# Attention feeding a feed-forward layer: one transposition earlier, one pair of loads swapped, one accumulation order regrouped

## The chip, the cores and the metric

The kernel runs on one core of one Trainium2 chip. The metric is the device time of one execution in microseconds (us). Three runs of the kernel before took 290.9, 291.38 and 291.52 us, median 291.38 us. The profiled execution of it spans 289.5 us; all times "at so many us" below are counted from the start of that span. The TensorE clock granted during it was 1.0 of full speed throughout.

Engine names as the profile gives them: PE is TensorE (matrix multiplication), PEld its weight loads, DVE is VectorE, ACT is ScalarE, POOL is GpSimd, SP is SyncE. SPq and POOLq stand for the queues from which transfers are issued.

## What is computed

Eight batches of attention with pooled keys and values, and then a feed-forward layer over all 4608 tokens:

```python
# q, k, v: 8 batches x 8 heads x 576 tokens x 64, float32
k_p = k.reshape(B, H, 72, 8, 64).mean(axis=3)      # 8 neighbours pooled: 72 keys
v_p = v.reshape(B, H, 72, 8, 64).mean(axis=3)
attn = softmax(q @ k_p.T / 8)                      # 576 x 72 for each head
x = (attn @ v_p)                                   # laid out as 4608 tokens x 512
h = x @ w_in                                       # 512 -> 2048
out = (h * sigmoid(h)) @ w_out                     # 2048 -> 512, float32
```

## The kernel before

The tokens are worked in nine **tiles** of 512 tokens, t = 0 to 8; attention is worked in eight **batches** of 576 tokens. In tile t the feed-forward layer is computed (`up`: the first product and the activation, then `down` or `down_quarters`: the second product), and batch a = t + 1 of the attention is slipped in between its matmuls. What is slipped in are "fillers": pairs of a step number and a function, where step i is the i-th matmul (or pair of matmuls) of the stage.

```python
def spread(fillers, n):
    todo = sorted(fillers, key=lambda f: f[0])
    for i in range(n):
        yield i                                  # the caller issues matmul i here
        while todo and todo[0][0] <= i:          # then the fillers due at step i
            todo.pop(0)[1]()
```

The order in which the program issues instructions is the order in which each engine gets them[...].

The second product of the first tile (t = 0) is plain. Its 512 tokens are four groups m = 0 to 3 of 128, with one PSUM bank for each group, and there are three such banks (`mm=3`), so groups 0, 1, 2 go together and group 3 takes the bank that group 0 leaves:

```python
def down(t, fillers, ms):                        # ms = [(0, 1, 2), (3,)]
    step = spread(fillers, KG * sum(len(mm) for mm in ms))      # KG = 16
    for mm in ms:
        o_ps = [ps_tile([128, d_model], FP32, "mm", "o_ps") for m in mm]
        for g in range(KG):                      # g: 16 slices of the 2048 hidden units
            for m, ps in zip(mm, o_ps):
                next(step)
                nc.tensor.matmul(ps, lhsT=h_T[:, g, m * 128 : (m + 1) * 128],
                                 rhs=w_out_sb[:, g, :],
                                 start=(g == 0), stop=(g == KG - 1))
        for m, ps in zip(mm, o_ps):
            copy = nc.vector.tensor_copy if m == 1 else nc.scalar.copy
            copy(o_sb[m // 2][:, m % 2, :], ps)
            store(t, m, slice(0, d_model))       # 4 transfers on SyncE's queue
```

Its fillers, by step of the 64 matmuls, are the attention of batch 1 (`a = 1`), and sums of weights for the later tiles:

```python
sc_at, den_at, nu_at = (1, 16, 30), (16, 30, 44), (44, 55, 56)   # t == 0
# scores: 16 matmuls, then 4 Exp on ACT;  denominators: 4 matmuls, then Ln, Exp on ACT
# numerators: 32 matmuls, then 2 multiplications on DVE that write xT for the next tile
f_down.append((37 + 3 * j, lambda j=j: select_v(1, j, "at")))    # 6 matmuls, j = 0, 1
f_down.append((37 + 3 * j, lambda j=j: copy_v(1, j)))            # 1 copy on DVE
# steps 48 to 55: weight_sum(1, ...) and weight_sum(3, ...), 8 additions on DVE
```

From t = 1 on the second product takes seven quarter products in place of eight (Strassen's scheme, in the variant of Winograd) and needs sums of hidden units on DVE:

```python
def down_quarters(t, fillers, last=False):       # 112 steps
    product(2, KA, KQ); product(5, KA, KQ); product(2, 0, KA)   # steps 0 to 23
    nc.scalar.copy(r_sb, ps["P"])
    product(5, 0, KA)                                           # steps 24 to 31
    tt(out=rr_sb, in0=ps["Q"], in1=r_sb, op=add)
    product(1, 0, KQ, cc)                                       # steps 32 to 47
    tt(out=t_sb[:, cs], in0=ps["R"][:, cs], in1=rr_sb[:, cs], op=sub)
    ...                                          # products 4, 3, 7 and 6, with copies and stores
```

The queries are transposed by four instructions of DVE for each batch, one for each half of the heads (n % 2) and half of the tokens (n // 2). In tile 1 three of them are in `up`, the fourth in `down_quarters`. It is needed by the scores of the second third of the tokens, at step 31:

```python
q_at = [15, 16, 17, 8] if t > 1 else [24, 25, 26, 8] if t else [82, 84, 86, 88]
for n in range(4):
    f_to = f_down if t and n == 3 else f_up
    f_to.append((q_at[n], lambda n=n: q_transpose(a, n % 2, n // 2)))
sc_at, den_at, nu_at = (1, 31, 75), (31, 56, 97), (56, 97, 101)        # t > 0
```

In tile 1 the values of batch 2 are pooled by six instructions of DVE (`slot_sums`, each half: two additions and one that writes the bf16 result), at step 8 as well, and issued ahead of the transposition because they were listed first. They are used at step 40:

```python
elif t == 1:
    for j in range(2):
        ...
        f_down.append((8, lambda j=j: slot_sums("v", j, halves=True)))
        f_down.append((40, lambda j=j: select_v(2, j, "at")))
        f_down.append((41, lambda j=j: copy_v(2, j)))
```

Batches 3 to 7 have their keys and values loaded in two parts: `load_one` writes the first four tokens of each eight through SyncE's queue, and `load_rest` adds the other four on top of it through GpSimd's queue, once the first part has landed. The queries go through GpSimd's queue, behind one another in the order of issue:

```python
elif a + 1 < B:                                            # t = 1 to 5
    f_up.append((0, lambda: load_q(a + 1)))                # nc.gpsimd.dma_start
    f_up.append((1, lambda: load_one(a + 1, "k")))         # nc.sync.dma_start, two of them
    f_up.append((2, lambda: load_rest(a + 1, "k")))        # nc.gpsimd.dma_start, adding
    f_down.append((11, lambda: load_one(a + 1, "v")))
    f_down.append((12, lambda: load_rest(a + 1, "v")))
```

Of the kernel before, what the change touches and what calls it, by code (L numbers as in the profile page):

```python
# [36 lines left out]
def kernel(  # L37
# [9 lines left out]
    nc = tc.nc  # L47
# [5 lines left out]
    d_model = H * D  # L53
    d_ff = moe_w_in.shape[1]
    KF = d_model // 128
    KG = d_ff // 128
# [118 lines left out]
    def load_one(b, name):  # L175
        st = batches.setdefault(b, {})
        raw = raw_tile(f"{name}_raw", H)
        load_rows(nc.sync, raw, source(b, name)[:, :, :PH])
        st[f"{name}_raw"] = raw
# [374 lines left out]
    def store(t, m, cs, engines=(nc.sync,)):  # L554
        n0 = (t * NTT + m * 128) // QP
        src = o_sb[m // 2][:, m % 2, cs]
        if n0 // QI == B - 1:
            engines[0].dma_start(out=out[n0 * QP : n0 * QP + 128, cs], in_=src)
            return
        for u in range(128 // QP):  # L560
            n = n0 + u
            rows = (
                out[n * QP : (n + 1) * QP] if n // QI == B - 1
                else out_r[n // QI, n % QI]
            )
            engines[u % len(engines)].dma_start(
                out=rows[:, cs], in_=src[QP * u : QP * (u + 1)]
            )


    def down(t, fillers, ms):
        step = spread(fillers, KG * sum(len(mm) for mm in ms))
        for mm in ms:
            o_ps = [ps_tile([128, d_model], FP32, "mm", "o_ps") for m in mm]
            for g in range(KG):
                for m, ps in zip(mm, o_ps):
                    next(step)
                    nc.tensor.matmul(  # L578
                        ps,
                        lhsT=h_T[:, g, m * 128 : (m + 1) * 128],  # L580
                        rhs=w_out_sb[:, g, :],
                        start=(g == 0), stop=(g == KG - 1),
                    )
            for m, ps in zip(mm, o_ps):
                copy = nc.vector.tensor_copy if m == 1 else nc.scalar.copy
                copy(o_sb[m // 2][:, m % 2, :], ps)  # L586
                store(t, m, slice(0, d_model))
        for _ in step:
            pass

# [194 lines left out]
    for t in range(NT):  # L785
        a = t + 1
        f_up, f_down = [], []
        if t == 0:
            GA = 11
            items = [(g, 0, HS) for g in range(GA)]  # L790
            items += [(g, HS, NTT - HS) for g in range(GA)]
            items += [(g, 0, NTT) for g in range(GA, KG)]
            f_up += [(1, lambda: denominators(0, part(0, 1), on_dve=True))]
            f_up += [(5, lambda: denominators(0, part(1, 1), on_dve=True))]
            f_up += [(13, lambda: numerators(0, part(0, 1)))]
            f_up += [(17, lambda: numerators(0, part(1, 1)))]
        else:
            G = lambda *gs: [(g, 0, NTT) for g in gs]
            if t == 1:
                items = (  # L800
                    G(12, 13, 14, 15) + [(0, "251")] + G(8) + [(0, "43")] + G(9)
                    + [(0, "76")] + G(10) + [(0, "s")] + G(11, 0, 1, 2, 3)
                )
            else:
                items = (
                    G(12, 13) + [(0, "251")] + G(14) + [(0, "43")] + G(15) + [(0, "76")]
                    + [(1, "2")] + [(0, "s")] + [(1, "51")] + G(0) + [(1, "43")] + G(1)
                    + [(1, "76")] + G(2) + [(1, "s")] + G(3)
                )
            for n in U_X:  # L810
                f_up.append((0, lambda n=n: unit_x_sum(t, n)))
            for n in (2, 5):
                f_up.append((36 if t > 1 else 45, lambda n=n: hidden_sum(n, 4, 8)))
            f_up.append((56, lambda: hidden_sum(6, 4, 8)))
            for n, k0 in ((2, 0), (5, 0), (1, 4), (1, 0)):
                f_up.append((64, lambda n=n, k0=k0: hidden_sum(n, k0, k0 + 4)))
            f_down.append((33, lambda: hidden_sum(7, 0, 8)))
            f_down.append((71, lambda: hidden_sum(6, 0, 4)))

        for n, t0, f_to, at, parts in (  # L820
            (1, 0, f_down, 48, (0, PW)), (3, 0, f_down, 52, (0, PW)),
            (4, 1, f_up, 38, (0, PW)), (7, 1, f_up, 42, (0, PW)),
            (6, 1, f_up, 60, (0, PW)),
        ):
            for i in range(*parts):
                if t == t0:
                    f_to.append((at + i, lambda n=n, i=i: weight_sum(n, i)))
        if a < B:
            q_at = [15, 16, 17, 8] if t > 1 else [24, 25, 26, 8] if t else [82, 84, 86, 88]
            if t == 0:  # L830
                for j in range(2):
                    f_up.append((44 + 8 * j, lambda j=j: slot_sums("k", j)))
                    f_up.append((72 + 8 * j, lambda j=j: select_k(1, j)))
                    f_up.append((72 + 8 * j, lambda j=j: copy_k(1, j)))
                    f_down.append((20 + 10 * j, lambda j=j: slot_sums("v", j)))
                    f_down.append((37 + 3 * j, lambda j=j: select_v(1, j, "at")))
                    f_down.append((37 + 3 * j, lambda j=j: copy_v(1, j)))
            elif t == 1:
                for j in range(2):
                    f_up.append((0, lambda j=j: slot_sums("k", j, halves=True)))  # L840
                    f_up.append((22, lambda j=j: select_k(2, j)))
                    f_up.append((23, lambda j=j: copy_k(2, j)))
# [3 lines that stand above are left out]
            else:  # L846
                f_up.append((22, lambda: k_transpose(a)))
                f_down.append((10, lambda: pool_v(a)))
# [3 lines that stand above are left out]
            if t == 0:  # L852
                f_down.append((0, lambda: load_half_2("k", 0)))
                f_down.append((0, lambda: load_q(2)))
                f_down.append((0, lambda: load_half_2("k", 1)))
                for half in range(2):
                    f_down.append((31, lambda half=half: load_half_2("v", half)))
                for y in range(2):
                    for n in U_W:
                        f_down.append((6, lambda y=y, n=n: unit_weight_sum(y, n)))  # L860
            elif a + 1 < B:
                for stage in range(2):
                    f_down.append((100, lambda stage=stage: pool_k(a + 1, stage)))
                f_up.append((0, lambda: load_q(a + 1)))
                f_up.append((1, lambda: load_one(a + 1, "k")))
                f_up.append((2, lambda: load_rest(a + 1, "k")))
                f_down.append((11, lambda: load_one(a + 1, "v")))
                f_down.append((12, lambda: load_rest(a + 1, "v")))
            f_down.append((0, attn_tables))

            if t:
                sc_at, den_at, nu_at = (1, 31, 75), (31, 56, 97), (56, 97, 101)
            else:
                sc_at, den_at, nu_at = (1, 16, 30), (16, 30, 44), (44, 55, 56)
            for n, sg in enumerate(visits):
                f_down.append((den_at[n], lambda sg=sg: denominators(a, sg)))
                f_down.append((sc_at[n], lambda sg=sg: scores(a, sg)))

            for n, sg in enumerate(visits):
                if n < 2 or not 0 < t < B - 2:  # L880
                    f_down.append((nu_at[n], lambda sg=sg: numerators(a, sg)))
                if n == 0 and 1 < t < B - 1:
                    f_down.append((nu_at[n], lambda: numerators(a - 1, visits[2])))
        moe_tables()
        up(t, f_up, items)
        if t == 0:
            down(t, f_down, [(0, 1, 2), (3,)])
        else:
            down_quarters(t, f_down, last=t == NT - 1)
# [28 lines left out]
```

The softmax here doesn't subtract the row's maximum and nothing guards it: scores larger than these inputs give would overflow.

## Time and profile before

| | before |
|---|---|
| time, median of 3 runs | 291.38 us |
| span of the profiled execution | 289.5 us |
| PE busy | 280.9 us, 97% |
| PE weight loads busy | 195.9 us, 68% |
| DVE busy | 225.6 us, 78% |
| ACT busy | 183.4 us, 63% |
| POOL busy | 52.3 us, 18% |
| HBM read and written | 36.70 MB and 9.44 MB |

Tile 0's `down` runs from 35.0 to 54.3 us, tile 1 from 54.3 to 86.7 us, and tiles 2 to 5 take about 29.4 us each (86.7 to 204.3 us). Tile 6 ends at 235.3 us. In tiles 7 and 8 there is no attention left.

To read it: a row of a timeline gives the start, the length in us, the engine, the line of the program, what is written and what it is made from, and in brackets how long the engine had been idle before it and which instruction ended that idle time. A matmul's end is modelled, and matmuls are pipelined, so that a PE row ends a little after the next one starts. A view of waits adds up such idle times by the pair of lines.

### The profile page before, as it was taken

To read this page: it belongs to the slowest core of one execution; us is meant where nothing else is said; L and a number is where in the kernel's file an instruction comes from. 1 tells how busy PE (TensorE), PEld (TensorE's weight loads), DVE (VectorE), ACT (ScalarE), POOL (GpSimd) and SP (SyncE) were. 2 spreads that over 40 slices of the span, in tenths; PEclk is the share of its full clock that TensorE was granted. 3 is DMA by queue.
4 is the path that set the end of the run, shared out by engine and by line. 5 is a ranking of instruction groups with operands and counts; after the bars stand their busy time and mean duration, and the time that the engine had idled before them with its cause. 6 is when DMAs were issued, how large, how long until landed. Compare 5 with 4: busy or idle time off the path is not lost.

```text
span 289.5 us, 6939 instructions
## 1 busy us (share of the span) xinstructions
PE 280.9 (97%) x2793; PEld 195.9 (68%) x2793; DVE 225.6 (78%) x403; ACT 183.4 (63%) x359; POOL 52.3 (18%) x68
## 2 busy tenths in 40 slices
PE   8999999999799999999999999999999999999995
PEld 3448544466586687668888876677566867786684
DVE  4887844979869797979698869986888876746783
ACT  1577676468466885778577957794678657425800
POOL 8654316401020012001020106203000000000000
PEclk9999999999999999999999999999999999999999
DMA  7999999794849563974969395979830023005004
GB/s 213 271 273 218 228 302 154 193 207 74 157 70 204 121 94 77 150 179 72 153 117 208 80 153 90 156 151 163 154 80 0 2 67 80 2 0 140 7 1 147
DMA packets 35296, 37.70 MB, mean 130 GB/s; under 512 B 9952, under 2 KB 27616, under 8 KB 35264
## 3 DMA queue, kind: packets, MB, share of 16 engines
q0 software_dynamic: 21760, 20.86, 43.1%
q1 hardware_dynamic: 12928, 15.48, 21.6%
q10 hardware_dynamic: 576, 0.92, 0.9%
q8 instruction: 22, 0.36, 0.5%
q14 instruction: 10, 0.08, 0.1%
HBM read 36.70 MB, written 9.44 MB: 159 GB/s over the span
## 4 chain that ended last, share of the span: by engine, by line
PE 87%; DVE 7%; ACT 3%; issue 1%; DMA 1%; SPq 0%; DVEq 0%
PE hp_ps L546 21%; PE o_psP L651 14%; PE o_psQ L651 14%; PE u_psQ L488 6%; PE u_psP L488 5%; PE o_psR L651 5%; PE o_ps L578 5%; PE warm_ps L700 4%; PE sc_ps L351 4%; PE nu_ps L395 3%; PE u_psR L488 2%; PE den_ps L369 2%; DVE h_sum L611 1%; DVE w_sum L629 1%; DVE qT L153 1%; DVE rr_sb L508 1%
## 5 line engine op out<-in xcount | busy, mean ns | idle before, releaser
L546 PE MATMUL hp_ps<-xT,w_in_sb 128*128 128x512 bf16 (+3 forms) x412 | 82.6, 340 | 0.4 <-ACT h_T L552 0.4
L552 ACT ACTIVATE h_T<-hp_ps 128x512 bf16<-128x512 f32 (+2 forms) x95 | 51.3, 545 | 27.6 <-PE hp_ps L546 26.5
L651 PEld LDWEIGHTS <-h_sum 128*128 128x128 bf16 x640 | 60.6, 98 | 11.9 <-issue 1.3
L611 DVE TENSOR_TENSOR h_sum<-h_T 128x1024 bf16<-128x1024 bf16 (+1 forms) x72 | 50.8, 742 | 7.0 <-ACT h_T L552 7.0
L546 PEld LDWEIGHTS <-w_in_sb 128*128 128x128 bf16 x412 | 39.3, 98 | 24.9 <-issue 1.5
L359 ACT ACTIVATE es<-sc_ps 72x384 bf16<-72x384 f32 (+1 forms) x100 | 39.1, 470 | 11.0 <-PE sc_ps L351 10.9
L488 PEld LDWEIGHTS <-w_sum 128*128 128x128 bf16 x300 | 29.3, 98 | 8.6 <-DVE x_sum L455 1.0
L651 PEld LDWEIGHTS <-h_T 128*128 128x128 bf16 x256 | 24.1, 98 | 4.4 <-issue 0.9
L496 ACT ACTIVATE h_T<-c_sb 128x512 bf16<-128x512 f32 x30 | 18.8, 628 | 11.6 <-DVE c_sb L520 11.6
L404 DVE TENSOR_TENSOR xT<-nu_ps,rec 128x384 bf16<-128x384 f32 (+1 forms) x50 | 24.0, 533 | 2.1 <-PE nu_ps L395 1.9
L378 ACT ACTIVATE lnd<-den_ps 128x384 f32<-128x384 f32 (+1 forms) x23 | 11.1, 484 | 21.2 <-PE den_ps L369 21.2
L153 DVE STREAM_TRANSPOSE qT<-q_bf 128x576 bf16<-128x576 bf16 x32 | 23.0, 754 | 0.2 <-DMA q_bf<-in_q_dram 0.2
L182 POOL DMA_DIRECT2D raw<-in_k_dram x5 | 7.0, 1404 | 70.5 <-DVE qT L153 33.2
L274 DVE TENSOR_TENSOR raw<-raw 128x384 f32<-128x384 f32 (+3 forms) x20 | 12.4, 618 | 7.6 <-DMA raw<-in_v_dram 4.3
L651 PE MATMUL o_psP<-w_out_sb,h_sum 128*128 128x256 bf16 x128 | 17.6, 273 | 0.0
L651 PE MATMUL o_psQ<-w_sum,h_sum 128*128 128x256 bf16 x128 | 16.7, 273 | 0.0
L651 PE MATMUL o_psQ<-w_out_sb,h_sum 128*128 128x256 bf16 x128 | 16.6, 273 | 0.0
L651 PE MATMUL o_psP<-w_sum,h_T 128*128 128x256 bf16 x128 | 16.5, 273 | 0.0
L651 PE MATMUL o_psQ<-w_sum,h_T 128*128 128x256 bf16 x128 | 16.5, 273 | 0.0
L578 PE MATMUL o_ps<-w_out_sb,h_T 128*128 128x512 bf16 x64 | 15.5, 380 | 0.6 <-ACT o_sb L586 0.6
L651 PE MATMUL o_psR<-w_sum,h_sum 128*128 128x256 bf16 x128 | 15.7, 273 | 0.0
L488 PEld LDWEIGHTS <-w_in_sb 128*128 128x128 bf16 x120 | 11.7, 97 | 5.7 <-issue 1.7
(77 smaller groups left out, 416.5 us busy)
## 6 DMA issues: line engine op xcount, KB each, us to landing
out_dram<-o_sb SPq DMA_DIRECT2D x128, 64.0 KB, 2.9
q_bf<-in_q_dram POOLq DMA_DIRECT2D x6, 576.0 KB, 11.4
raw<-in_k_dram SPq DMA_DIRECT2D x6, 512.0 KB, 5.3
raw<-in_k_dram POOLq DMA_DIRECT2D x5, 576.0 KB, 9.2
raw<-in_v_dram POOLq DMA_DIRECT2D x5, 576.0 KB, 9.3
raw<-in_v_dram SPq DMA_DIRECT2D x5, 512.0 KB, 6.2
w_in_sb<-in_moe_w_in_dram POOLq DMA_DIRECT2D x8, 256.0 KB, 8.3
w_out_sb<-in_moe_w_out_dram POOLq DMA_DIRECT2D x4, 512.0 KB, 13.7
```

Of the source, the lines that this page charges most:

```text
L153: nc.vector.transpose(out=st["qT"][:, a, f * QF : (f + 1) * QF].rearrange("r i c p -> r (i c p)"), in_=st["q_bf"][:, a, f * n : (f + 1) * n],)
L274: nc.vector.tensor_add(out=raw[..., :w], in0=raw[..., :w], in1=raw[..., w : 2 * w])
L351: nc.tensor.matmul(sc[s][:, cs], lhsT=kz[b % 2][rows, g, c, :], rhs=st["qT"][rows, g, i0:i1, c, :], start=(c == 0), stop=(c == 1),)
L359: nc.scalar.activation(es[:, s, :], sc[s], func=AF.Exp, scale=score_scale)
L404: nc.vector.tensor_mul(out=xT[:, 2 * g0 + c : 2 * (g0 + ng - 1) + c + 1 : 2, cols], in0=nu[c][:, :w].rearrange("r (g n) -> r g n", g=ng), ...
L488: nc.tensor.matmul(ps[bank][:, u, :], lhsT=w[:, kk, 128 * u : 128 * (u + 1)], rhs=x[:, kk, :], start=first and u == 0 and kk == 0, stop=kk ...
L496: nc.scalar.activation(h_T[:, g : g + 2, j * NQ : (j + 1) * NQ], src, func=AF.Silu)
L546: nc.tensor.matmul(hp_ps[:, r0:r1], lhsT=w_in_sb[:, kk, g * 128 : (g + 1) * 128], rhs=xT[:, kk, x0 : x0 + r1 - r0], start=(kk == 0), stop= ...
L552: nc.scalar.activation(h_T[:, g, n0 : n0 + n], hp_ps[:, :n], func=AF.Silu)
L578: nc.tensor.matmul(ps, lhsT=h_T[:, g, m * 128 : (m + 1) * 128], rhs=w_out_sb[:, g, :], start=(g == 0), stop=(g == KG - 1),)
L611: nc.vector.tensor_tensor(out=h_sum[n][:, ks, :], in0=quarter(*a, ks), in1=quarter(*b, ks), op=op)
L651: nc.tensor.matmul(ps[b][:, c, :], lhsT=left(n, kt, c), rhs=W_OUT[n][:, kt, :], start=b not in begun, stop=kt == k1 - 1, skip_group_check= ...
```

## The change: what it does and what it is for

Three edits. The number of instructions and the work of each stay the same.

- In tile 0 the last quarter of the second product (g = 12 to 15) is done group by group in place of slice by slice, and each group is copied out and stored as soon as its own last matmul is issued. It is for letting groups 0 and 1 leave their banks while PE still works on groups 1 and 2.
- In tile 1 the fourth transposition of the queries moves from step 8 to step 2 of the second product, which puts it ahead of the sums of the values on DVE. It is for having the queries ready when the scores of the second third want them.
- In tiles 1 to 5 the first part of the next keys is issued one step ahead of the next queries, in place of one step after. It is for having the keys, which are needed first, asked for first.

```diff
--- before.py
+++ after.py
@@ def down
-            for g in range(KG):
-                for m, ps in zip(mm, o_ps):
-                    next(step)
-                    nc.tensor.matmul(
-                        ...
-                    )
-            for m, ps in zip(mm, o_ps):
-                copy = nc.vector.tensor_copy if m == 1 else nc.scalar.copy
-                copy(o_sb[m // 2][:, m % 2, :], ps)
-                store(t, m, slice(0, d_model))
+            last = KG - KG // 4
+            for g, (m, ps) in (
+                [(g, x) for g in range(last) for x in zip(mm, o_ps)]
+                + [(g, x) for x in zip(mm, o_ps) for g in range(last, KG)]
+            ):
+                next(step)
+                nc.tensor.matmul(
+                    ...
+                )
+                if g == KG - 1:
+                    copy = nc.vector.tensor_copy if m == 1 else nc.scalar.copy
+                    copy(o_sb[m // 2][:, m % 2, :], ps)
+                    store(t, m, slice(0, d_model))
@@ fillers of each tile
-            q_at = [15, 16, 17, 8] if t > 1 else [24, 25, 26, 8] if t else [82, 84, 86, 88]
+            q_at = [15, 16, 17, 8] if t > 1 else [24, 25, 26, 2] if t else [82, 84, 86, 88]
@@
-                f_up.append((0, lambda: load_q(a + 1)))
-                f_up.append((1, lambda: load_one(a + 1, "k")))
+                f_up.append((0, lambda: load_one(a + 1, "k")))
+                f_up.append((1, lambda: load_q(a + 1)))
```

More of the change, by code (lines that the diff above doesn't have):

```diff
@@ L574, in down @@
             o_ps = [ps_tile([128, d_model], FP32, "mm", "o_ps") for m in mm]
-            for g in range(KG):
-                for m, ps in zip(mm, o_ps):
-                    next(step)
[L578 to L582, printed above, removed]
-                    )
-            for m, ps in zip(mm, o_ps):
-                copy = nc.vector.tensor_copy if m == 1 else nc.scalar.copy
-                copy(o_sb[m // 2][:, m % 2, :], ps)
-                store(t, m, slice(0, d_model))
+            last = KG - KG // 4
[5 more added lines that the diff above has]
+                nc.tensor.matmul(
+                    ps,
+                    lhsT=h_T[:, g, m * 128 : (m + 1) * 128],
+                    rhs=w_out_sb[:, g, :],
+                    start=(g == 0), stop=(g == KG - 1),
+                )
[3 more added lines that the diff above has]
+                    store(t, m, slice(0, d_model))
         for _ in step:
```

## The prediction

> **What bounds the kernel now.** I first read the page's busy times: PE is busy for 97% of the span, nothing else for more than 78%. PE ends are modelled, so that alone is weak. I therefore asked which waits of PE itself are recorded (columns: us in total, times, longest us):
>
> ```profile
> PE sc_ps L351 <- DVE qT L153: 1.8, 2, 1.5
> PE warm_ps L700 <- DVE warm L713: 1.2, 1, 1.2
> PE u_psR L488 <- DVE x_sum L455: 0.7, 1, 0.7
> PE o_ps L578 <- ACT o_sb L586: 0.6, 1, 0.6
> PE hp_ps L546 <- ACT h_T L552: 0.4, 1, 0.4
> ```
>
> The reader is to see how short this list is: 4.7 us in 289.5. PE is the bound, and a change that does not shorten PE's work can at most remove such waits. The first line (1.5 of it) and the fourth are those that the change is aimed at. Next, the timeline at these two places. In tile 0, PE stops before the fourth group:
>
> ```profile
> 47.73 0.35 PE L369 MATMUL den_ps<-es,ones 72*32 72x384 bf16 x4
> 48.34 0.82 PE L578 MATMUL o_ps<-w_out_sb,h_T 128*128 128x512 bf16 x3
> 48.37 1.02 DVE L404 TENSOR_TENSOR xT<-nu_ps,rec 128x384 bf16<-128x384 f32 x2 [1.08 <-PE nu_ps L395]
> 48.73 0.52 ACT L379 ACTIVATE rec<-lnd 128x384 f32<-128x384 f32 x1
> 49.16 1.06 ACT L586 COPY o_sb<-o_ps 128x512 f32<-128x512 f32 x2
> 49.31 0.68 DVE L586 COPY o_sb<-o_ps 128x512 f32<-128x512 f32 x1
> 49.78 1.89 PE L578 MATMUL o_ps<-w_out_sb,h_T 128*128 128x512 bf16 x8 [0.62 <-ACT o_sb L586]
> ```
>
> The eight matmuls at 49.78 are group 3; they wait for ACT to empty group 0's bank, and ACT is late because group 0 ended only three matmuls ago, and because Ln and Exp of the denominators stand ahead of the copy. In tile 1:
>
> ```profile
> 72.76 0.55 DVE L274 TENSOR_TENSOR raw<-raw 128x384 f32<-128x384 f32 x1
> 73.34 0.36 DVE L278 TENSOR_TENSOR v<-raw 128x192 bf16<-128x192 f32 x1
> 73.62 0.42 DVE L274 TENSOR_TENSOR raw<-raw 128x256 f32<-128x256 f32 x1
> 74.07 0.29 DVE L278 TENSOR_TENSOR v<-raw 128x128 bf16<-128x128 f32 x1
> 74.28 0.77 DVE L153 STREAM_TRANSPOSE qT<-q_bf 128x576 bf16<-128x576 bf16 x1
> 75.11 0.36 PE L351 MATMUL sc_ps<-qT,kz 32*72 32x192 bf16 x8 [1.52 <-DVE qT L153]
> ```
>
> PE has done half of the scores by 73.58 and stands still for 1.52 us, while DVE sums values that PE needs only at 76.39 (v_ps in the same timeline). DVE is the late one: it has no gap between 61.08 and 76.75, so its order decides. Last, the stretches of the steady tiles (stretch, its length, then busy times of PE, PEld, DVE, ACT and POOL, clock, share of the DMA engines, GB/s):
>
> ```profile
> 86.70:116.10 29.40, 29.29 (x315) 21.47 (x313) 25.33 (x43) 21.41 (x42) 3.54 (x3) 1.00 0.61 124
> ...
> 174.90:204.30 29.40, 29.29 (x315) 21.47 (x313) 24.73 (x42) 21.41 (x42) 9.54 (x11) 1.00 0.95 139
> 204.30:235.30 31.00, 30.15 (x331) 21.53 (x329) 26.41 (x44) 21.99 (x42) 0.00 (x0) 1.00 0.27 57
> ```
>
> Tiles 2 to 5 take the same 29.4 us, with PE busy for all but 0.1: whatever is gained before 86.7 should be carried through them unchanged.
>
> [...] the queries for batch 2 were asked for at 37.6 and need some 11.4 us, so they were there by about 49, yet the transposition ran at 74.28, behind the sums; PE's later matmuls did not pass the waiting one. [...]
>
> **The change part by part.**
>
> *Regrouping in tile 0.* No matmul is added or removed. Group 0 now ends at step 39, which before ran near 46.2. ACT is idle from 46.25 (end of the Exp rows) to 48.21, so the copy of some 0.55 us fits in that gap and the bank is free near 46.9, two microseconds ahead of need. PE then has no reason to stop: three matmuls issued at 48.34 at 0.216 us apiece (15 took 3.34 us in the chain, 0.22 each) end their issue at 48.99, so group 3 starts near 49.0 and not at 49.78: 0.79 us. On DVE the copy of group 1 (0.68 us) moves ahead of the first multiplications, into DVE's idle 1.08 us before 48.37: DVE then runs in one piece to the end of the multiplications that write xT, at 54.54 before, and so gains about 0.64 us, all but the overlap of neighbouring rows. Tile 1's first matmuls need xT: they started at 54.33 with the second held to about 54.55. After: PE arrives near 53.5, xT is complete near 53.9. The smaller gain counts: **0.65 us**.
>
> *The transposition.* DVE reaches this point at 72.76, less 0.65 that is 72.1. The transposition comes first, 0.77 us: ready at about 72.9. PE arrives at 73.58 less 0.65, 72.93. The wait of **1.5 us** vanishes. What moves back are four rows of sums, 0.55 + 0.36 + 0.42 + 0.29, some 1.5 us as spaced in the timeline: they end near 74.4. Their user, v_ps, stood 1.0 us behind the start of o_psR (75.40 to 76.39) and would now come at 73.25 + 1.0 = 74.25 for the first half, whose sums are done at 73.8, and 74.6 for the second, done at 74.4. No wait. Next, DVE has rr_sb (0.65), a sum of hidden units (1.2) and the two copies of v_ps (0.75): 74.4 + 2.5 gives 76.8 to 76.9. PE wants these copies for the numerators, at 79.04 before, 2.15 earlier now, at 76.9. This is a tie, worth at most 0.1 us of new wait. Behind it DVE had 0.8 to 1.6 us idle, and recovers.
>
> *Keys ahead of queries.* `load_one` goes out on SyncE's queue, `load_q` and `load_rest` on GpSimd's. The two swapped neighbours stand on different queues, and each queue's own order stays: SP still has stores, then keys; POOL still has queries, then the rest of the keys. I expect **0**.
>
> Sum: 0.65 + 1.5 - 0.05 = 2.1 us; 291.38 - 2.1 = 289.3.
>
> **The rivals.**
>
> *First, DVE takes over as the bound in tile 1 and gives only part back.* For it: DVE's unbroken 15 us there, and the tie at 76.9. Against it: DVE idles for 0.82, 1.64 and 1.11 us before its next three waits on PE (79.50, 82.76, 84.56). It would cost 0.1 to 0.6 us: 289.4 to 289.9.
>
> *Second, transfers eat the gain.* The record of landings gives the ends of `load_rest` for the keys of batches 3 to 7 as 77.2, 110.1, 143.9, 173.4 and 204.69; DVE's first addition on them starts at 86.12, 115.49, 144.86, 174.26 and 204.72. The reserve shrinks: 8.9, 5.4, 0.9, 0.8 and none, and the last one waited:
>
> ```profile
> DVE raw L188 <- DMA raw<-in_k_dram: 1.0, 1, 1.0
> PE u_psR L488 <- DVE x_sum L455: 0.7, 1, 0.7
> ```
>
> If the landings stayed where they are, the wait in tile 6 would grow by the whole 2.1 and the time would be near 291. Against it: these keys are issued behind the stores of the tile before (85.28 in tile 2, right after the first result of DVE), so the chain starts from compute and moves with it, and the DMA engines fall idle in each tile (0.1 or less of their share at 100 to 104, 132 to 136, 162 to 166), so no backlog crosses a tile. One piece does not move: the first part of the values of batch 3 waits for the first half of the sums of the values, at 73.7 before and near 73.8 after, so it and the queries behind it then overlap tile 1's stores by 2 us more. The reserve of 5.4 us in tile 2 should absorb that; a remnant could cost some tenths in tiles 3 to 6.
>
> *Third, the wait in tile 0 is only renamed*, PE stopping for xT at the boundary: already counted (0.79 cut to 0.65). If DVE gained nothing there, 0.65 would be lost: 290.0.
>
> **Range and chances.** Both aimed-at waits vanish, less 0.1 for transfers: 289.4 us. Low: 288.7, if the wait in tile 6 also goes. High: 290.7, if most of the gain is held up by transfers; the runs before spread by 0.6. A gain of 2% would be 5.8 us, more than all waits of PE together (4.7), and a loss of 2% needs a new stall in several tiles; I give 0.01 to each, 0.98 to within 2%.
>
> **What would show it.** Right: no wait of o_ps for ACT; scores in tile 1 waiting under 0.2 us for qT; tile 1 starting 0.6 to 0.8 earlier and ending about 2.1 earlier; tiles 2 to 5 at 29.4 us; POOL and SP in the same order. Wrong: a wait of PE for vp or for rr_sb in tile 1, tiles 3 to 6 longer, the addition on the keys waiting for DMA in more than one tile or for over 1 us, or keys landing relatively earlier (the third part at work after all).

## The result, and the profile after

The changed kernel took 288.91 us (median of 6 runs, 287.84 to 289.22) against 291.45 us for the kernel before on the same chip (6 runs, 290.9 to 293.18). The ratio is 0.9898, 95% interval 0.9868 to 0.9929: about 1% faster, under 2%. The ratio agrees with the means (288.66 over 291.62), and one of the six runs of before, at 293.18, makes it look better than the medians do. The kernels were timed in four sets, each on one chip with its own runs of before. Over all sets there are 20 executions of the changed kernel (this set, e4 and e11 below; why e4 counts as the same kernel is shown there), with a mean of 288.85 us, and in the three later sets 131 of before, with a mean of 291.22 us: **2.37 us** gained, interval 2.09 to 2.64 from resampling both groups. I use this below as the measured gain. It is not exact to a few tenths: set by set the means give 3.0 us (here), 2.6 us (e4) and 1.9 us (e11).

TensorE's own waits after, the five longest (us in total, times, longest):

```profile
PE warm_ps L703 <- DVE warm L716: 1.2, 1, 1.2
PE hp_ps L546 <- ACT h_T L552: 0.4, 1, 0.4
PE warm_ps L703 <- issue: 0.3, 2, 0.2
PE sc_ps L351 <- DVE qT L153: 0.3, 1, 0.3
PE u_psR L488 <- ACT r_sb L505: 0.2, 1, 0.2
```

The wait of o_ps for ACT is gone, and of the 1.8 us for qT 0.3 is left, which lies at 17.3 us in the prologue (what runs ahead of tile 0's second product). The timeline of the end of tile 0 after:

```profile
46.50 0.59 ACT L589 COPY o_sb<-o_ps 128x512 f32<-128x512 f32 x1
...
47.80 0.69 DVE L589 COPY o_sb<-o_ps 128x512 f32<-128x512 f32 x1 [0.33 <-PE o_ps L581]
...
48.52 2.55 PE L581 MATMUL o_ps<-w_out_sb,h_T 128*128 128x512 bf16 x10
48.55 1.02 DVE L404 TENSOR_TENSOR xT<-nu_ps,rec 128x384 bf16<-128x384 f32 x2
...
52.17 1.94 DVE L404 TENSOR_TENSOR xT<-nu_ps,rec 128x384 bf16<-128x384 f32 x4
```

Group 0 is copied at 46.50, two microseconds ahead of need; the last three matmuls of group 2 and the first eight of group 3 are one row without a gap (one of the eleven records is missing from the trace). In tile 1:

```profile
72.23 0.77 DVE L153 STREAM_TRANSPOSE qT<-q_bf 128x576 bf16<-128x576 bf16 x1
...
72.69 0.72 PE L351 MATMUL sc_ps<-qT,kz 32*72 32x192 bf16 x16
...
73.34 1.16 PE L654 MATMUL o_psR<-w_sum,h_sum 128*128 128x256 bf16 x9
...
74.34 0.69 PE L314 MATMUL v_ps<-v,shifts 128*72 128x64 bf16 x12
...
76.14 0.75 DVE L321 CAST vp<-v_ps 72x256 bf16<-72x256 f32 x2
...
76.98 0.50 PE L395 MATMUL nu_ps<-es,vp 72*32 72x192 bf16 x16
```

DVE ran the transposition in its new place in the program, at 72.23 and ahead of the sums, where before ran it at 74.28 and behind them. All 16 score matmuls run in one row, o_psR starts at 73.34 in place of 75.40, and the copies vp are done at 76.89, just in time for the numerators at 76.98. The steady stretches stay as they were, and the wait for the keys of batch 7 became smaller in this execution (first two lines: the stretches with the columns of before; third: DVE's wait):

```profile
84.65:114.05 29.40, 29.19 (x313) 21.50 (x313) 25.33 (x43) 21.41 (x42) 1.66 (x2) 1.00 0.73 133
172.85:202.25 29.40, 29.18 (x312) 21.47 (x313) 24.77 (x43) 21.41 (x42) 9.54 (x11) 1.00 0.94 136
```

```profile
DVE raw L188 <- DMA raw<-in_k_dram: 0.6, 1, 0.6
```

For all kernels I took stage lengths from the traces, between the first matmuls of the second products of successive tiles (d0 is tile 0's, and so on), in us:

| kernel | start to d0 | d0 to d1 | d1 to d2 | d2 to d3 | d3 to d6 | d6 to end |
|---|---|---|---|---|---|---|
| before | 35.04 | 33.64 | 31.51 | 29.37 | 89.24 | 70.67 |
| changed | 35.22 | 32.92 | 29.99 | 29.37 | 88.79 | 70.67 |
| regrouping alone | 34.42 | 32.92 | 31.51 | 29.37 | 88.74 | 70.68 |
| transposition alone | 34.47 | 33.64 | 29.98 | 29.36 | 89.04 | 70.67 |
| swap alone | 34.15 | 33.64 | 31.51 | 29.37 | 88.88 | 70.66 |
| changed without swap | 34.88 | 32.92 | 29.98 | 29.37 | 89.00 | 70.66 |
| before, queries late | 34.51 | 33.64 | 31.51 | 29.37 | 88.15 | 70.67 |
| regrouping again | 34.82 | 32.93 | **33.03** | 29.37 | 89.68 | 70.67 |
| regrouping, queries late | 34.30 | 32.92 | 31.50 | 29.37 | 88.14 | 70.68 |
| changed, queries late | 34.19 | 32.92 | 29.98 | 29.37 | 88.13 | 70.66 |

Two columns move from execution to execution whatever the kernel: the prologue by up to 1.1 us, and tiles 3 to 6, by the waits for keys. The prologue goes with the moment at which TensorE gets its full clock: in before the matmuls of 128x512 start every 0.43 us up to 6.8 us, and every 0.22 us after it. (The mean clock of 1.0 given for before counts this first stretch as full, since the trace's record of the clock begins with the release.) In the 14 profiles the release comes at 4.1 to 7.2 us; the prologue takes 34.15 to 34.51 us where it comes before 5.8 us, and 35.22 and 35.24 us where it comes at 7.1 and 7.2 us. The columns d0 to d2 are exact to 0.02 us, and hold the two aimed-at effects: **0.72 us** for the regrouping, **1.52 us** for the transposition, each the same alone and together. One cell, in bold, is out of line; it led to what I had not seen.

### The profile page after: what moved, and what is told of

It reads as the page before. It is cut to its first block, busy times and chain, and to the rows that moved or that the text cites. A ratio compares the mean times of both kernels' runs of the same rounds, so it can differ in the third digit from the quotient of the medians.

```text
span 287.0 us, 6919 instructions
## 1 busy us (share of the span) xinstructions
PE 279.4 (97%) x2773; PEld 196.0 (68%) x2793; DVE 225.6 (79%) x403; ACT 183.4 (64%) x359; POOL 52.6 (18%) x68
## 4 chain that ended last, share of the span: by engine, by line
PE 91%; DVE 4%; ACT 2%; issue 1%; DVEq 0%
PE hp_ps L546 23%; PE o_psP L654 15%; PE o_psQ L654 15%; PE u_psQ L488 7%; PE u_psP L488 6%; PE o_psR L654 5%; PE sc_ps L351 4%; PE warm_ps L703 4%; PE o_ps L581 3%; PE nu_ps L395 3%; PE den_ps L369 2%; PE u_psR L488 2%; DVE rr_sb L508 1%; ACT r_sb L505 1%; DVE w_sum L632 1%
## 5 line engine op out<-in xcount | busy, mean ns | idle before, releaser
L546 PE MATMUL hp_ps<-xT,w_in_sb 128*128 128x512 bf16 (+3 forms) x397 | 80.8, 338 | 1.4 <-ACT h_T L552 0.4
L546 PEld LDWEIGHTS <-w_in_sb 128*128 128x128 bf16 x412 | 39.3, 98 | 24.9 <-issue 1.4
L182 POOL DMA_DIRECT2D raw<-in_v_dram x5 | 6.9, 1390 | 49.4 <-DMA raw<-in_v_dram 15.6
L558 POOL DMA_DIRECT2D out_dram<-o_sb x1 | 0.6, 628 | 81.8 <-issue 81.8
```

The costliest lines, as they stand in the source:

```text
L182: nc.gpsimd.dma_start(out=batches[b][f"{name}_raw"], in_=source(b, name)[:, :, PH:], accum_op=ALU.add,)
L546: nc.tensor.matmul(hp_ps[:, r0:r1], lhsT=w_in_sb[:, kk, g * 128 : (g + 1) * 128], rhs=xT[:, kk, x0 : x0 + r1 - r0], start=(kk == 0), stop= ...
```

## The experiments

**Each part alone, and the change without the swap.** Theory: the gain is the sum of two removed waits, the swap is nothing. Rivals: transfers take it back, or the swap moved the keys.

```diff
# e2, on before:
-            q_at = ... else [24, 25, 26, 8] if t else ...
+            q_at = ... else [24, 25, 26, 2] if t else ...
# e3, on before:
-                f_up.append((0, lambda: load_q(a + 1)))
-                f_up.append((1, lambda: load_one(a + 1, "k")))
+                f_up.append((0, lambda: load_one(a + 1, "k")))
+                f_up.append((1, lambda: load_q(a + 1)))
# e1: before with the new loop of down() alone; e4: changed, with e3's edit taken back
```

> Regrouping in tile 0 alone. If the gain is the sum of the removed waits of TensorE: no wait of o_ps for ScalarE, tile 1 starts 0.7 us earlier against tile 0's second product, the 1.5 us wait of the scores in tile 1 stays as it was (both its sides move), and the kernel gains 0.7 us. If instead the gain needs both edits together (rival): under 0.3 us.

> The transposition in tile 1 alone. Sum of waits: the scores in tile 1 wait under 0.2 us, tile 1 becomes 1.5 us shorter, the wait of 0.6 us in tile 0 stays, the kernel gains 1.5 us, or up to 2.0 us if the keys' transfer in tile 6 also comes in time. Rival, transfers: the landing of the keys of batch 7 stays where it is, TensorE's wait in tile 6 grows from 0.7 to 2.2 us, and nothing is gained.

> Keys ahead of queries alone. If the swap changes nothing on any queue: time within 0.2% of before, and the first addition on the keys of batch 7 waits for its transfer between 0.5 and 1.2 us as before. Rival, the swap is what brought the keys of batch 7 earlier in the changed kernel: that wait falls to 0.6 us or less and the kernel gains 0.3 to 0.5 us.

> Regrouping and transposition without the swap. If the swap does nothing: the same time as the changed kernel, 2.2 to 2.7 us under before, tile 6 as in the changed kernel within 0.4 us. If the swap brought the keys earlier: 0.4 us slower than the changed kernel, with the 1.0 us wait for the keys of batch 7 back.

| kernel | median us (runs) | ratio to before, interval |
|---|---|---|
| e1 regrouping | 290.88 (22) | 0.9996, 0.9976 to 1.0016 |
| e2 transposition | 289.11 (14) | 0.9942, 0.9923 to 0.9962 |
| e3 swap | 291.00 (14) | 1.0000, 0.9979 to 1.0020 |
| e4 without swap | 288.60 (6) | 0.9936, 0.9916 to 0.9957 |

Before had 291.14 us here (43 runs). The swap does nothing. The traces of before and e3 show the same operations on VectorE and ScalarE and the same transfers issued by GpSimd and SyncE, each in the same order, and so do those of the changed kernel and e4; so I count e4 as the changed kernel. The times agree with this, but their interval of 0.2% either way, some 0.6 us, could not by itself have excluded the 0.3 to 0.5 us of the rival. The wait for the keys of batch 7 was 0.62 us in e3, inside the band expected of no effect but next to the rival's 0.6. In e4 none was recorded for these keys, where the rival had 1.0 us, but one of 0.58 us for those of batch 5. These waits move between executions of the same kernel, and the smaller wait in the changed kernel's first profile was scatter. The transposition brings 0.6%, some 1.7 to 2.0 us. The regrouping is a miss: its trace shows the 0.72 us, its times show next to nothing. Its 22 times spread from 289.28 to 292.9, and 11 of them have a mean granted TensorE clock of 0.993 or 0.994 (median 291.8 us), while the other 11 have 0.998 or 1.0 (median 289.97 us).

**The same kernel once more, and the queries out of the way of the keys.** The label of the second expectation, e6, says "qlate", yet the kernel is the regrouping alone, unchanged. In the others the queries are issued behind the second part of the keys on the same queue, which, unlike the swap, does change the order of issue: in before the next queries go out at 81.83 us and the second part of the keys at 101.36, in the trace of e8 this part at 99.41 and the queries at 100.23.

```diff
-                f_up.append((0, lambda: load_q(a + 1)))
-                f_up.append((1, lambda: load_one(a + 1, "k")))
+                f_up.append((0, lambda: load_one(a + 1, "k")))
+                f_up.append((3, lambda: load_q(a + 1)))     # load_rest of the keys is at 2
```

> The kernel before, with the next queries issued behind the second part of the next keys on the same queue (tiles 1 to 5)[...]. Theory, the keys' transfers bind tiles 3 to 6: no wait for them is left, the stretch from the second product of tile 3 to that of tile 6 falls from 89.2 to about 88.3 us, 0.9 us gained in the median. Rival, the waits in tiles 3 to 6 are made by DVE's load and not by the transfers: nothing gained. Risk: the queries of batch 7 come late, and tile 6 grows.

> The regrouping alone once more, one look. If the missing gain of the first run of it (0.26 us in the median in place of 0.7) is lost to transfers: tile 0 and tile 1 as in its first profile (18.5 us and 18.1 us from the start of tile 0's second product to tile 1, and from tile 1's second product to tile 2), and waits for keys in tiles 3 to 6 of another size than the 0.6 us seen. If it is lost in tiles 0 to 2: one of those two is longer.

> The regrouping alone, with the next queries behind the second part of the next keys. If transfers hid its gain: 0.7 us under the kernel before with late queries, 1.6 us under before, with fewer slow executions. If regrouping itself gives less than its trace shows: under 0.3 us between those two.

> The changed kernel with the next queries behind the second part of the next keys. If the keys' transfers are the only thing left between the sum of the two removed waits and the measured time: no wait for keys, 2.2 us under the kernel before with late queries, about 288.1 us. Rival, the queries come late for tile 6: a new wait of DVE for q_bf there, and 289 us or more.

The second profile of the regrouping is of an execution of 292.42 us whose mean clock is 0.993. Its span is 2.9 us longer than that of the first profile: 1.52 us of this lie in tile 1, 0.94 in the waits for keys of tiles 3 to 6, and 0.40 in the prologue. The stretches in tile 1 (stretch, length, busy times of PE, PEld, DVE, ACT, POOL, then the granted clock, DMA share, GB/s) show where the 1.52 us come from:

```profile
72.00:73.00 1.00, 0.65 (x13) 0.32 (x13) 0.97 (x3) 0.49 (x1) 0.00 (x0) 1.00 0.82 123
73.00:74.00 1.00, 0.00 (x0) 0.00 (x0) 0.97 (x3) 0.52 (x1) 0.00 (x0) 1.00 0.91 138
74.00:75.00 1.00, 0.83 (x12) 0.55 (x12) 1.00 (x3) 0.47 (x2) 0.00 (x0) 0.80 1.02 164
75.00:76.00 1.00, 1.00 (x6) 0.74 (x5) 0.82 (x1) 1.00 (x4) 0.00 (x0) 0.50 1.02 263
76.00:77.00 1.00, 1.00 (x14) 0.91 (x11) 0.00 (x0) 0.14 (x1) 0.00 (x0) 0.50 1.03 202
77.00:78.00 1.00, 1.00 (x7) 0.70 (x6) 0.65 (x2) 0.00 (x0) 0.00 (x0) 0.50 0.68 136
78.00:79.00 1.00, 1.00 (x11) 0.87 (x10) 0.52 (x2) 0.00 (x0) 0.00 (x0) 0.99 0.07 12
```

PE stands still for the transposition from 72.64 to 74.17; 0.4 us later the clock falls to half for 3.4 us, which lowers the mean of the whole execution by 0.006. Below I count each execution with a mean of 0.994 or less as one with a fall; where the fall lay was seen in this one alone. So the stall costs its 1.5 us and, in some executions, another 1.5 us.

The late queries settle the transfers. Before with late queries: 289.9 us against 291.35 (22 and 43 runs), ratio 0.9952, 0.9935 to 0.9968; no wait for keys, d3 to d6 88.15 in place of 89.24, as expected; the gain of 1.4 us is more than the 0.9 expected. The regrouping with late queries: 288.97 us (22 runs), ratio 0.9939, 0.9919 to 0.9959. Fourteen of its runs have full clock and a median of 288.77, 1.1 us under before with late queries; eight have 0.994 and a median of 290.94. The expected 0.7 is there, and more (its profile has 0.72 of it in tile 0 and 0.2 in the prologue), but the low clocks are there too. Transfers had not hidden it: in e1 as well, the executions of full clock (0.998 or 1.0) average 1.2 us under those of before in the same set. The changed kernel with late queries: 287.76 us (6 runs), ratio 0.9888, 0.9852 to 0.9923, where I had expected about 288.1. Neither it nor before with late queries has a low clock or a wait for keys, so the difference of their means, 2.19 us (1.8 to 2.5), is the cleanest measure of the two removed waits, 0.72 + 1.52 = 2.24. In the changed kernel with late queries, DVE goes from one addition to the next without a wait for the keys of batch 7:

```profile
199.60 1.02 DVE L404 TENSOR_TENSOR xT<-nu_ps,rec 128x384 bf16<-128x384 f32 x2
200.54 1.21 DVE L188 TENSOR_TENSOR raw<-raw 72x1024 f32<-72x1024 f32 x1
```

**Is it TensorE's standing still that lowers the clock?** The stall is filled with needless matmuls on zeros, or made longer; the changed kernel and the one with late queries run beside.

```diff
# e9, on the regrouping alone, in down_quarters ahead of rr_sb:
+        if t == 1:
+            for _ in range(12):
+                nc.tensor.matmul(ps["R"][:, 0, :], lhsT=warm[:, :128], rhs=warm[:, :256],
+                                 start=True, stop=True, skip_group_check=True)
# e10, on the regrouping alone:
-            q_at = ... else [24, 25, 26, 8] if t else ...
+            q_at = ... else [24, 25, 26, 31] if t else ...
```

> The regrouping alone, and in tile 1, ahead of the scores that wait for the transposition, 12 matmuls on zeros (128x256, 1.3 us) into a bank that is not yet in use: work that the kernel doesn't need, in the time in which TensorE would stand still. Theory, TensorE's clock falls to half for 3.4 us[...]: no execution with a granted clock of 0.994 or less is left (half and a third of the executions had it with the regrouping alone), the slow group of times at 291 to 292 us vanishes, and the median falls from 290.9 to about 290.0 us. Rival, the lower clock has another cause than TensorE's idle time: the same share of executions has it.

> The regrouping alone, and the transposition in tile 1 behind rr_sb as well, so that TensorE stands still for 2.1 us and not 1.5. Theory of the clock: more executions than with the regrouping alone have a granted clock of 0.994 or less, over half. The median rises by more than the 0.65 us of the longer stall, to 292 us. Rival, the stall costs only its length: 290.6 us in the median of those with full clock, and no more executions with the lower clock than before.

> The changed kernel again, beside the next one on the same chip. 288.3 to 289.0 us, no execution with a clock of 0.994 or less, waits for keys of 0.4 to 0.9 us in all in tiles 3 to 6.

> The changed kernel with the next queries behind the second part of the next keys, again. 287.5 to 288.0 us, 0.5 to 0.9 us under the changed kernel, no wait for keys.

Filled (timeline), and longer:

```profile
71.37 1.47 PE L671 MATMUL o_psR<-warm 128*128 128x256 bf16 x12
...
73.63 0.36 PE L351 MATMUL sc_ps<-qT,kz 32*72 32x192 bf16 x8 [0.22 <-DVE qT L153]
```

```profile
74.19 0.36 PE L351 MATMUL sc_ps<-qT,kz 32*72 32x192 bf16 x8 [2.12 <-DVE qT L153]
```

| kernel | runs | with a clock of 0.994 or less |
|---|---|---|
| before, three later sets | 131 | 14 |
| regrouping alone, both | 23 | 12 |
| regrouping, stall filled | 22 | 0 |
| regrouping, longer stall | 22 | 12 |
| regrouping, queries late | 22 | 8 |
| before, queries late | 22 | 0 |
| swap alone | 14 | 1 |
| transposition moved (changed, e2, e4, e8, e11, e12) | 46 | 0 |

The tile with the filled stall takes exactly as long (d1 to d2 31.52 us), and the low clock is gone: 0 of 22 against 12 of 23, and against 12 of 22 with the longer stall, timed beside it on the same chip. That is the cause shown: TensorE's standing still there brings the fall. In before, the 14 executions with a low clock average 292.53 us and the other 117 291.06 us, so that a fall costs 1.47 us, as in the trace.

The median of the filled kernel, 290.77 us, missed my 290.0, though: ratio 0.9989, 0.9970 to 1.0008, against 290.7 for before in that set. Over all sets it stands 0.53 us under before (0.23 to 0.83), where the stages say 0.72 and the avoided falls 0.2 more; within its own set, its mean is no lower than that of the executions of before with full clock. Tiles 3 to 6 took 88.96 us in its profile, so waits for keys are there, but I can't split the rest: that the filled kernel keeps the regrouping's 0.72 is shown by its stages, and not by its times. The longer stall kept over half of its runs at the low clock, as expected, but no larger share than the shorter one; its median rose to 291.9 us, ratio 1.0028, 1.0005 to 1.0050. Those of its runs with a clock above 0.994 have a median of 290.68 us, which is what the rival said. The share rising with length is not shown.

The changed kernel again: 289.03 us (8 runs), ratio 0.9926, 0.9894 to 0.9958, with the waits for keys at another place:

```profile
DVE raw L188 <- DMA raw<-in_k_dram: 1.0, 2, 0.8
```

I had expected 0.4 to 0.9 us of waits and a time of at most 289.0 us. With late queries again: **287.56 us** (6 runs, 287.2 to 287.95), ratio 0.9875, 0.9840 to 0.9911, the quickest kernel here. It beats the changed one by 1.5 us in this set, where I had expected 0.5 to 0.9, and over all sets by 1.2 us of the means (287.65 against 288.85); the removed waits for keys account for 0.7 to 1.2 of that (88.13 against 88.79, 89.00 and 89.33 us).

## Why the prediction was off, point by point

*The size.* I forecast 289.4 us, a gain of 2.0. The median of 288.91 lies inside the range, but the ratio of 0.9898 stands for 3.0 us (2.1 to 3.8), and 0.9898 times 291.45, 288.5 us, lies below my low end of 288.7. Over all executions the gain is 2.37 us; the other 0.6 of the first set I take for scatter, since its runs of before average 0.4 us above the pooled mean and those of the changed kernel 0.2 below. The two waits went as worked out; the sum lacked a term.

*Regrouping: right.* 0.65 predicted, 0.72 measured. Group 3 starts without a gap. Of the 0.79 worked out for it 0.07 is lost up to tile 1's second product; I had put 0.14 down to xT at the boundary.

*Transposition: right as far as it went.* 1.5 predicted, 1.52 measured; v_ps came at 74.34 (predicted 74.25), the copies vp at 76.14 to 76.89 (76.8 to 76.9), and the tie at 76.9 cost nothing visible.

*Keys ahead of queries: right.* 0 predicted, ratio 1.0000 measured. The edit is aimed at a real shortage (before waited 1.0 us for the keys of batch 7), but swaps neighbours on different queues.

*The step that failed: "Sum: 0.65 + 1.5 - 0.05".* It prices a stall at its length. The stall in tile 1 also pulls TensorE's clock down (to 0.50 in the one trace that holds a fall) in some executions: 14 of 131 of before have the low clock, and none of 46 with the transposition moved. One fall cost 1.52 us in its trace, so 14/131 of that, 0.16 us, vanishes in the mean: 0.72 + 1.52 + 0.16 = 2.40 against the 2.37 measured. Of the 0.4 us by which my 2.0 falls short of this sum, 0.16 is the missing term, 0.15 are the deductions for the tie (0.05) and for transfers (0.1), which were not due, and 0.09 are the sizes of the two waits. That the sum comes within 0.03 of the measured gain is luck, as the sets differ by up to 1.1 us. I had taken the clock of 1.0 in the one profile for a property of the kernel. It also explains the regrouping alone: 12 of 23 runs with the fall in place of 14 of 131 is 0.42 more falls a run, 0.6 us at 1.52 each (in e1 the medians of the two groups lie 1.8 apart, which makes it 0.8), which eats the 0.72. The two edits are not additive in time, only in stages: without the transposition the regrouping is worth 0.3 us in the mean (e1, and 0.3 again with late queries), neither of them clear of noise.

*The second rival: half right.* The reserve of the keys in tile 2 fell from 5.4 to between 0.5 and 2.6 us in the three profiles of the changed kernel, and in two of the three DVE then waited 0.6 and 0.8 us for the keys at the end of tile 3. That it fell for the reason given is not shown: with the regrouping alone, where the first part of the values moves along with the rest, it was 1.9 us in one profile and 5.7 in the other. But tiles 3 to 6 lose about as much in before (89.24 and, as the swap alone, 88.88, against 88.79, 89.00 and 89.33): 0.7 to 1.2 us over the 88.14 that late queries reach. So the 0.1 deducted for transfers was not due, and a gain was left lying there.

*The first rival* did not appear: no wait of PE for vp or rr_sb. *The third* was priced right.

*The low end of the range* was tied to tile 6's wait alone. It should have been set lower for the prologue too, which moved by 1.1 us between profiles, and by 0.9 between two of the same order of instructions (before and the swap).

## What to carry to other kernels

A stall of the bounding engine should be looked for in the clock column behind it, in several executions and not in one: here filling 1.5 us of idle time or removing it also removed the low clock (0 of 22 and 0 of 46 runs, against 12 of 23). A single edit whose times come in two groups should be split by granted clock before it is called useless. And to have one transfer go ahead of another, change the order within one queue: here queries issued behind the keys took away the waits for keys in tiles 3 to 6, and 1.4 us (289.9 against 291.35 us), while swapping the lines of two queues in the program moved nothing (291.0 against 291.14 us).

## What the runs showed of the hardware

The fall of the clock came after a stall of 1.52 us between small matmuls: in that trace the granted clock was 0.50 from about 74.6 to 78.0 us, 3.4 us in all, and 1.00 again from 79 us on. The 13 other profiles have a mean granted clock of 0.999 or 1.0, and none has a fall. Six of them have the stall unfilled: five of 1.5 us, and the one with the longer stall of 2.12 us. So the length of the standstill alone does not tell the trace with the fall from those without. What does is not shown, with one trace of a fall.

Why the regrouping alone has a fall in half of its runs and before in a tenth stays open as well. Measured were 20 of 45 (the regrouping, with early and late queries), 14 of 131 (before) and 12 of 22 (the longer stall). The stall of before comes 0.72 us later; whether that matters is not shown, as no run moved the stall and left the rest as it was. Before with late queries had no fall in 22 runs; a rate of one in ten gives that about one time in twelve.
